# Staging the output weight of linear attention over freed operands, by GpSimd's queue, in a two-branch mixer

## The chip, the cores and the metric

The kernel runs on one core of one Trainium2 chip. The metric is the device time of one execution in microseconds (us); before the change three runs gave a median of 617.96 us, the lowest 616.56 and the highest 618.06.

## What is computed

From one input x of 2048 rows and 512 columns the reference computes `x + A(layernorm(x)) + B(layernorm(x))`, everything in float32. A is linear attention with 32 heads of 16 columns, B a gated MLP that mixes over the rows:

```python
# A: linear attention with a learned feature map
q, k, v = split(x @ wqkv)
phi_q = concat(softmax(q @ w_phi), softmax(-q @ w_phi))      # phi_k in the same way
kv, z = phi_k^T v, sum over rows of phi_k
o = (phi_q kv) / (phi_q z + 1e-6)
A = o @ wo                                                    # wo: 512 x 512
# B: gated MLP
z1, z2 = halves of gelu(x @ w_in)                             # 688 columns each
g = w_sp @ layernorm(z2) + b_sp
B = (z1 * g) @ w_out                                          # w_out: 688 x 512
```

## The kernel before

Every float32 operand of a matmul is split into a rounded high part and a rest (`round_h` on ACT, `rest_l` on DVE), and `mm3` issues three matmuls for one product. Rows are worked in 16 blocks of 128. A first stage projects q, k and v, forms the softmax features and adds up kv and z; the unnormalised q features of each block go to DRAM (`e_d`), as do the z1 halves (`z1_d`). A second stage makes z2 and splits it into the right operands B of the spatial product. A third stage computes `w_sp @ z2` in 8 pairs of output blocks times 4 quarters of the sum (`SEQ`, `products`); a drain (`drain`, L801 to L814) takes the sums out of PSUM, `gate` multiplies them with gelu(z1), and the transposed result u goes to DRAM. In the last pair the quarters run in the order 1, 2, 3, 0, so that the right operands of the second quarter (number 1) are dead first and those of the first quarter (number 0) last.

The last stage works on the blocks two at a time, i = 0, 2, ... 14. `project_u` multiplies u by w_out (tile `pout`), `attend` multiplies the features with kv and splits the outcome into `oT`, `project_o` multiplies `oT` with wo into the same `pout` and stores it: for most blocks ACT copies it to `xr` and GpSimd's queue adds it to the output, which already holds x (L1041). `features(s)` finishes the q features of block s: `q_fin` (L560 to L571) on DVE, from a load by `load_q` (tile `et`, L557). Blocks below 8 are turned by PE (`ptq`, L989), the later ones by DVE and a way through DRAM, which brings them back in pairs (`f`, L954). `ahead(i)` issues loads and features some blocks ahead.

What the change touches:

- SBUF is a stack. The right operands B of the third stage lie in tiles of one pool after another: the first quarter's in the pool `xz2a` and the first two tiles of `xz2`, the second quarter's in the last three tiles of `xz2` and in others. `stage_w` (L876) puts the raw rows of w_out into three tiles of `xz2` as they come free and splits them (tiles `wof` and `wu`, L49 and L53). When the third stage closes, the pool `cw` of the last stage takes the same addresses, in the order in which its tiles are first named (L961 to L967); a tile waits only for the users of the addresses under it.
- The raw rows of wo (tiles `wof`, one for each of 4 quarters of 128 rows) are loaded at L1056 to L1058 by SP, in 4 pieces of 32 rows each, so 16 DMAs, and split at once into `woh` and `wol`. The block at L1055 keeps ACT's and DVE's splits behind the split of u of block 1 (`uh`, `ul`) and behind `q_fin` of block 2 on their engines.
- Behind the wo loads (`load_w.last`) the block at L1059 puts, on SP, the features' load of block 3 (et(3)), the u of blocks 2 and 3, and et(4). `features(3)` follows `attend(0)` on DVE.
- `load_z1(7)`, the last pair's z1, is written at L1097 in step i = 2 and sent by GpSimd. The block around it names `lasts[6]`, an instruction of DVE (the last of `features`), and such a block orders only instructions of the same engine; so nothing holds the load back on GpSimd's queue.
- `er_pair` gives the pairs of turned features from a tag with 3 buffers.

The order on each engine is otherwise made by a planner, which simulates the program and takes what is ready first; instructions then run in that order on their engine or queue.

Of the kernel before, what the change touches and what calls it, by code (L numbers as in the profile page):

```python
# [10 lines left out]
F32 = mybir.dt.float32  # L11
F32R = mybir.dt.float32r
AF = mybir.ActivationFunctionType
ALU = mybir.AluOpType
# [4 lines left out]
P = 128  # L19
S, D, H, DH, FH = 2048, 512, 32, 16, 688  # L20
NT = S // P
ND = D // P
FC = FH // 2
NG = 4
NF = 2 * D
KF = FH // P
# [8 lines left out]
HP, QP = P // 2, P // 4  # L35
FP = 3 * P
# [5 lines left out]
def mixer(ctx: ExitStack, tc: tile.TileContext, x, x_t, wv, wqkT, phi_bd, wo, w_in, wst, b_r, w_out, out):  # L42
    nc = tc.nc
    pe, act, dve, pool, sp = nc.tensor, nc.scalar, nc.vector, nc.gpsimd, nc.sync


    def round_h(eng, h, src):
        if eng is act:
            return act.activation(h, src, AF.Copy).ins  # L49
        return eng.tensor_copy(h, src).ins  # L50

    def rest_l(l, src, h, eng=None):
        return (eng or dve).tensor_tensor(l, src, h.bitcast(F32), op=ALU.subtract).ins  # L53

    def mm3(dst, a, b, start, stop):
        (ah, al), (bh, bl) = a, b
        pe.matmul(dst, ah, bh, start=start, stop=False)  # L57
        pe.matmul(dst, ah, bl, start=False, stop=False)  # L58
        return pe.matmul(dst, al, bh, start=False, stop=stop).ins  # L59
# [12 lines left out]
    def xz_tile(n, dt, name):  # L72
        return xz.tile([P, SL], dt, tag="xz", name=name)[:, :n]
# [121 lines left out]
    with ExitStack() as p0:  # L195
# [16 lines left out]
        def split_w(h, l, src, t):  # L212
            sp.dma_start(t, src)
            round_h(act, h, t)
            rest_l(l, t, h)
# [134 lines left out]
        def proj_k(s):  # L350
            er = (spare[s] or stage("er")).rearrange("p a b -> p (a b)")[:, :NF + 2 * H] if s in spare else None
            return softmax_pair(wk, proj(s, wqk_h[:, 1], wqk_l[:, 1]), "k", r_x[:, s:s + 1], er=er)
# [79 lines left out]
        t = xz_tile(2 * D, F32R, "xT").rearrange("p (a b) -> p a b", a=2)  # L432
# [8 lines left out]
        for cs, pt in zip(halves, pts):  # L441
            src = pt.rearrange("p a b -> p (a b)")
# [63 lines left out]
        for s in range(NT):  # L506
# [6 lines left out]
            er = ek[s] if s < len(ek) else proj_k(s)  # L513
# [46 lines left out]
    def q_fin(et, tmp, zb):  # L560

        e, r, t, w = et[:, :NF], *(et[:, NF + k * 2 * H:NF + (k + 1) * 2 * H] for k in range(3))
        den = et[:, NF + 6 * H:QW]
        dve.tensor_tensor(tmp, e, zb, op=ALU.mult)
        dve.tensor_reduce(t, heads(tmp), axis=AX.X, op=ALU.add)
        dve.tensor_tensor(t, t, r, op=ALU.mult)
        dve.scalar_tensor_tensor(den, pairs(t, 0), EPS_DEN, pairs(t, 1), op0=ALU.add, op1=ALU.add)
        dve.reciprocal(den, den)
        dve.tensor_tensor(w.rearrange("p (h a) -> p h a", a=2), r.rearrange("p (h a) -> p h a", a=2),
                          den.unsqueeze(2).to_broadcast([P, H, 2]), op=ALU.mult)  # L570
        return e, dve.tensor_tensor(heads(e), heads(e), bc(w, 2 * H), op=ALU.mult).ins  # L571
# [6 lines left out]
    def turn_q(s, dst, e, eng):  # L578

        dve.transpose(dst.rearrange("p (m c t) -> p m c t", c=NB, t=BL), e.rearrange("p (c m j) -> p m c j", c=NB, j=BL))  # L580
        for b in range(P // BL):
            eng.dma_start(q_d[s, :, b * QB:(b + 1) * QB].rearrange("(m j) w -> j m w", j=BL),
                          dst[b * BL:(b + 1) * BL].rearrange("p (m w) -> p m w", w=QB))
# [154 lines left out]
    for s in range(NT):  # L738
# [8 lines left out]
        for k, q in p:  # L747
            ins = act.activation(z[(slice(None), *k)], q, AF.Gelu_apprx_tanh, scale=r_x[:, s:s + 1]).ins
# [95 lines left out]
    def slot(name, dt=F32):  # L844
        return xz_tile(2 * FH, dt, name)

    def load_w(src, parts, h, l, t):
        rows = 0
        for r0, r1 in parts:
            load_w.last = sp.dma_start(t[rows:rows + r1 - r0], src[r0:r1, :]).ins  # L850
            rows += r1 - r0
        return round_h(act, h, t[:rows]), rest_l(l, t[:rows], h)

    def load_u(i, u, rt):
        sp.dma_start(u, u_d[i])
# [18 lines left out]
    lasts, wu = [None] * 9, []  # L874

    def stage_w():  # L876
        t = [xz2.tile([P, SL], F32, tag="b", name="wof") for _ in range(3)]
        w = [xz_tile(2 * D, F32R, "wu") for _ in range(KF + 1)]
        for c in range(KF + 1):
            n = P if c < KF else 2 * REM  # L880
            h, l = (w[c][:n, k * D:(k + 1) * D] for k in range(2))
            rows = [(c * P, (c + 1) * P)] if c < KF else [(KF * P, FH)] * 2
            load_w(w_out, rows, h, l, t[c // 2][:, c % 2 * D:(c % 2 + 1) * D])
            wu.append((h, l))

    g, es, ets, ft, brought = {}, {}, {}, {}, {}
    for n in range(NC):
# [4 lines left out]
        if n % NQ == NQ - 1 and i < NP - 1:  # L892
            c = gt.tile([P, 2, FU], F32, tag="c", name="c")
# [7 lines left out]
        if n % NQ == NQ - 1 and i < NP - 1:  # L901
# [3 lines left out]
            if i in (2, 4):  # L905
                s = i // 2 - 1
                e, t = (gt.tile([P, 2, FU], F32, tag=tag, name=name).rearrange("p k f -> p (k f)")[:, :NF]
                        for tag, name in (("c", "c"), ("z1", "z1t")))
                pool.dma_start(e, e_d[s, :, :NF])
                turn_q(s, t, e, pool)  # L910
        if n == NC - 4:
            stage_w()
# [6 lines left out]
        if n == NC - 2:  # L919
# [4 lines left out]
            t = xz_tile((KF + 1) * P, F32R, "u1")  # L924
# [9 lines left out]
    cw = ctx.enter_context(left("cw", 1))  # L934
# [4 lines left out]
        return load_u(i, cw.tile([P, KF * P], F32, tag="u", bufs=4, name="u"),  # L939
                      cw.tile([2 * REM, P], F32R, tag="rt", bufs=6, name="rt"))  # L940

    def er_pair(name):
        return cw.tile([P, 2, NF], F32, tag="er", bufs=3, name=name)

    def features(s):
        with tc.issue_after(fin[-1]):
            tmp = slot("qtmp")[:, :NF]
            es[s], ins = q_fin(ets.pop(s), tmp, zb)
        fin.append(ins)
        if s >= TQ:  # L950
            if s % 2 == 0:
                ft[s] = er_pair("f")
            turn_q(s, tmp, es.pop(s), pool)
            brought[s] = sp.dma_start(ft[s - s % 2][:, s % 2], q_d[s]).ins  # L954
            return
        lasts[6] = ins

    def gated(u):
        return split_u(*u, wk.tile([P, KF, P], F32R, tag="uh", name="uh"), wk.tile([P, KF, P], F32R, tag="ul", name="ul"))

    er_pair("er")  # L961
    wo_h = cw.tile([P, ND, D], F32R, name="woh")
    cw.tile([2 * REM, P], F32R, tag="rt", bufs=6, name="rt")
    cw.tile([P, D], F32, tag="wof", bufs=4, name="wof")
    kvT = cw.tile([P, 2 * NG, HP], F32, name="kvT")
    cw.tile([P, KF * P], F32, tag="u", bufs=4, name="u")
    wo_l = cw.tile([P, ND, D], F32R, name="wol")  # L967
    with tc.issue_after(cb[1]), tc.issue_after(cb[2]):
        uT.append(gated(us.pop(1)))
    ctx_psg.__exit__(None, None, None)  # L970
# [50 lines left out]
    def project_o(i, oT, p):  # L1021
        ts = slice(i % 2 * P, (i % 2 + 1) * P)
        rows = slice(i * P, (i + 1) * P)
        xr = wk.tile([P, D], F32, tag="xr", bufs=3, name="xr")
        if i >= NT - 2:
            sp.dma_start(xr, x[rows, :])
        if i == NT - 1:
            dve.tensor_tensor(xr, p, xr, op=ALU.add)
            parts = [(slice(k * D // 2, (k + 1) * D // 2), pst.tile([P, D // 2], F32, tag="tr", name="pend")) for k in range(2)]
        else:  # L1030
            parts = [(slice(0, D), p)]
        for cs, q in parts:
            for c in range(ND):
                lasts[4] = mm3(q, (oT[0][:, c, ts], oT[1][:, c, ts]), (wo_h[:, c, cs], wo_l[:, c, cs]),
                               q is not p and c == 0, c == ND - 1)
            if i == NT - 2:
                dve.tensor_tensor(xr, p, xr, op=ALU.add)
                sp.dma_start(out[rows, :], xr)
            elif q is p:
                act.activation(xr, p, AF.Copy)  # L1040
                ins = pool.dma_start(out[rows, :], xr, accum_op=ALU.add).ins  # L1041
                tc.add_manual_dep(ins, seeds[i].name, mybir.DependencyInfo(
                    mybir.DependencyClass.Sync, mybir.DependencyReason.DATA), reason="out holds x")
            else:
                dve.tensor_tensor(xr[:, cs], q, xr[:, cs], op=ALU.add)
                sp.dma_start(out[rows, cs], xr[:, cs])
# [7 lines left out]
    wk.tile([P, NG, 2 * P], F32R, tag="oTh", name="oT")  # L1054
    with tc.issue_after(lasts[0]), tc.issue_after(lasts[1]), tc.issue_after(fin[-1]):  # L1055
        for c in range(ND):  # L1056
            rows = [(m * QP, (m + 1) * QP) for m in range(c // 2 * 8 + c % 2, (c // 2 + 1) * 8, 2)]
            load_w(wo, rows, wo_h[:, c], wo_l[:, c], cw.tile([P, D], F32, tag="wof", bufs=4, name="wof"))  # L1058
    with tc.issue_after(load_w.last):  # L1059
        ets[3] = load_q(3, slot("et"))  # L1060
        for s in (2, 3):
# [3 lines left out]
    def ahead(i):  # L1065

        if i + 5 < NT:
            ets[i + 5] = load_q(i + 5, slot("et"))
        if i + 4 < NT:
            with tc.issue_after(brought[i + 2]) if i + 6 >= NT else ExitStack():  # L1070
                us[i + 4] = fetch_u(i + 4)
        if 3 < i + 3 < NT:
            features(i + 3)
# [64 lines left out]
```

## Time and profile before

| what | value |
|---|---|
| median of the runs (lowest to highest) | 617.96 us (616.56 to 618.06) |
| the profiled execution's own time | 615.26 us |
| its span, first to last instruction | 613.6 us |
| PE busy | 606.3 us (99%) |
| DVE, ACT, POOL busy | 519.9, 259.9, 132.4 us |
| granted clock of PE | 1.00 |
| moved by DMA | 107.85 MB, mean 176 GB/s |

In the lines shown below, L49 is a cast to the high part, L53 the rest on DVE, L57 to L59 the three matmuls of `mm3`. A row of a timeline gives the start in us from the span's start, the length (of all, where rows are merged: x2, x4), engine and line, operation, tile written and tiles read, shapes, and in brackets how long the engine sat idle before it and what ended that. "SPq" is the queue of SyncE, whose rows are the issues of DMAs and not their transfers. Waits are given as total, times, longest. A row of a stretch gives from:to, its length, the busy time of PE, PEld, DVE, ACT and POOL with the number of instructions, PE's granted clock, the busy share of the 16 DMA engines and GB/s. A row of the DMA issues gives count, KB each and the median us from issue to landing.

### The profile page before, as it was taken

The numbers are of one execution on the slowest core, as the hardware profiler recorded it, in microseconds if no ns is written. First come the engines' busy times: TensorE is split into PE (matmuls) and PEld (weight loads), VectorE is DVE, ScalarE is ACT, GpSimd is POOL, SyncE is SP. The second block draws the span as 40 slices with busy tenths as digits, with TensorE's granted clock in tenths as the row PEclk, the third lists the DMA queues.
The fourth block names the chain that finished last, engine by engine and source line by source line (L and its number), as shares of the span: only waits on it lengthen the run. The fifth ranks groups of instructions, "written<-read, shape, count | busy, mean of one in ns | idle before, by whom it ended". The sixth has DMA issues, their size and how long they took to land.

```text
span 613.6 us, 11385 instructions
## 1 busy us (share of the span) xinstructions
PE 606.3 (99%) x4286; PEld 551.5 (90%) x4286; DVE 519.9 (85%) x930; ACT 259.9 (42%) x414; POOL 132.4 (22%) x231
## 2 busy tenths in 40 slices
PE   8999999999999999999999999999999999999997
PEld 7888888888888999999999999999999978777776
DVE  5999999999988588999989897787779979999932
ACT  5653334423433547887434443332435243332220
POOL 4122232333111014542000002001100131053440
PEclk9999999999999999999999999999999999999999
DMA  8557776666547848001454746455566798599882
GB/s 309 196 135 170 224 174 183 153 161 171 134 120 206 275 155 308 2 1 35 150 135 133 193 100 182 132 158 145 162 179 215 239 312 253 150 293 278 222 221 67
DMA packets 57950, 107.85 MB, mean 176 GB/s; under 512 B 12392, under 2 KB 24552, under 8 KB 57672
## 3 DMA queue, kind: packets, MB, share of 16 engines
q1 hardware_dynamic: 43656, 65.22, 34.5%
q0 software_dynamic: 11936, 36.28, 24.0%
q10 hardware_dynamic: 2304, 5.64, 2.4%
q8 instruction: 33, 0.54, 0.4%
q14 instruction: 21, 0.17, 0.1%
HBM read 66.85 MB, written 35.54 MB: 167 GB/s over the span
## 4 chain that ended last, share of the span: by engine, by line
PE 83%; DVE 6%; DMA 6%; issue 2%; SPq 1%; ACT 1%; POOL 0%; ACTq 0%; DVEq 0%; POOLq 0%
PE g L57 8%; PE g L58 8%; PE g L59 8%; PE proj L58 7%; PE proj L57 7%; PE proj L59 7%; PE zps L58 6%; PE zps L59 6%; PE zps L57 6%; PE pout L57 5%; PE pout L59 5%; PE pout L58 5%; DVE A L53 2%; DMA wf<-in_wst 1%; PE po L1004 1%
## 5 line engine op out<-in xcount | busy, mean ns | idle before, releaser
L57 PE MATMUL g<-B,A 128*128 128x344 f32 x448 | 142.5, 319 | 0.3 <-DVE c L810 0.3
L58 PE MATMUL g<-B,A 128*128 128x344 f32 x448 | 142.4, 319 | 0.0
L59 PE MATMUL g<-B,A 128*128 128x344 f32 x448 | 138.9, 318 | 0.0
L57 PEld LDWEIGHTS g<-B,A 128*128 128x128 f32 x448 | 84.0, 188 | 0.9 <-DVE c L810 0.6
L58 PEld LDWEIGHTS g<-B,A 128*128 128x128 f32 x448 | 84.0, 188 | 0.0
L59 PEld LDWEIGHTS g<-B,A 128*128 128x128 f32 x448 | 83.6, 188 | 0.0
L49 ACT ACTIVATE A<-S 128x512 fp32r<-128x512 f32 x64 | 39.4, 628 | 70.7 <-DVE S L622 52.3
L57 PE MATMUL proj<-wqk_h,xT 128*128 128x512 f32 x128 | 50.1, 391 | 0.0
L59 PE MATMUL proj<-wqk_h,xT 128*128 128x512 f32 x128 | 49.8, 389 | 0.0
L58 PE MATMUL proj<-wqk_l,xT 128*128 128x512 f32 x128 | 49.8, 389 | 0.0
L125 ACT ACTIVATE e<-e,r_x 128x1024 f32<-128x1024 f32 x26 | 29.8, 1149 | 42.3 <-DVE e L124 41.3
L53 DVE TENSOR_TENSOR A<-S,A 128x512 fp32r<-128x512 f32 x64 | 43.0, 684 | 3.0 <-ACT A L49 2.8
L49 ACT ACTIVATE A<-wf 128x512 fp32r<-128x512 f32 (+1 forms) x64 | 32.8, 515 | 28.1 <-DMA wf<-in_wst 15.8
L57 PE MATMUL zps<-w1h,xT 128*128 128x344 f32 (+2 forms) x128 | 40.8, 320 | 0.0
L59 PE MATMUL zps<-w1h,xT 128*128 128x344 f32 (+2 forms) x128 | 40.7, 318 | 0.0
L58 PE MATMUL zps<-w1l,xT 128*128 128x344 f32 (+2 forms) x128 | 40.7, 318 | 0.0
L57 PE MATMUL zps<-w2h,xT 128*128 128x344 f32 (+2 forms) x128 | 40.7, 318 | 0.0
L58 PE MATMUL zps<-w2l,xT 128*128 128x344 f32 (+2 forms) x128 | 40.6, 317 | 0.0
L59 PE MATMUL zps<-w2h,xT 128*128 128x344 f32 (+2 forms) x128 | 40.3, 317 | 0.0
L53 DVE TENSOR_TENSOR A<-wf,A 128x512 fp32r<-128x512 f32 (+1 forms) x64 | 35.1, 550 | 4.1 <-ACT A L49 4.0
L787 POOL DMA_DIRECT2D z1t<-z_d x16 | 8.7, 550 | 132.5 <-DMA wf<-in_wst 98.1
L128 DVE TENSOR_REDUCE sm<-e 128x64 f32<-128x1024 f32 x26 | 31.1, 1199 | 2.5 <-ACT e L125 2.5
(219 smaller groups left out, 1434.4 us busy)
## 6 DMA issues: line engine op xcount, KB each, us to landing
wf<-in_wst SPq DMA_DIRECT2D x64, 256.0 KB, 3.4
e_d<-e POOLq DMA_DIRECT2D x16, 544.0 KB, 5.0
et<-e_d SPq DMA_DIRECT2D x16, 544.0 KB, 7.6
z_d<-z1f ACTq DMA_DIRECT2D x16, 344.0 KB, 3.1
z1t<-z_d POOLq DMA_DIRECT2D x16, 344.0 KB, 4.6
zacc<-e POOLq DMA_DIRECT2D x10, 512.0 KB, 4.8
u<-u_d SPq DMA_DIRECT2D x15, 320.0 KB, 5.8
xt<-in_x SPq DMA_DIRECT2D x16, 256.0 KB, 4.4
```

The source lines that it names most:

```text
L49: return act.activation(h, src, AF.Copy).ins
L53: return (eng or dve).tensor_tensor(l, src, h.bitcast(F32), op=ALU.subtract).ins
L57: pe.matmul(dst, ah, bh, start=start, stop=False)
L58: pe.matmul(dst, ah, bl, start=False, stop=False)
L59: return pe.matmul(dst, al, bh, start=False, stop=stop).ins
L125: softmax_pair.last = less, act.activation(e, e, AF.Exp, scale=scale).ins
L128: dve.tensor_reduce(sm, heads(e), axis=AX.X, op=ALU.add)
L787: pool.dma_start(t[:, k, :FH], z1_d[2 * i + k])
L1004: lasts[3] = pe.matmul(po[r][c * QP:(c + 1) * QP, k], kvT[rows, m // 2, cols], fs[m // 4][rows, m // 2 % 2], start=True, stop=True).ins
```

## The change

The raw rows of wo get their place and their loads earlier in the code, right where the last stage's pools open. Three of the four quarters go out on GpSimd's queue (`eng=pool`), the last on SP's. The order of the tiles in `cw` is new: the pairs of turned features and the u buffers come first and lie over the first quarter's operands, as does `wol`; `wof` lies over two tiles in which the second quarter's operands lay, and after them the staging of w_out; `woh` lies over further tiles that the third stage has freed. `load_w` only loads, `split_w` only splits; the splits of wo stay where they were. The pairs of turned features get 2 buffers instead of 3. `lasts[6]` is now the last adding store of the output on GpSimd's queue, so that the last z1 load is queued behind it.

```diff
-    def load_w(src, parts, h, l, t):
+    def load_w(src, parts, t, eng=sp):
         rows = 0
         for r0, r1 in parts:
-            load_w.last = sp.dma_start(t[rows:rows + r1 - r0], src[r0:r1, :]).ins
+            load_w.last = eng.dma_start(t[rows:rows + r1 - r0], src[r0:r1, :]).ins
             rows += r1 - r0
-        return round_h(act, h, t[:rows]), rest_l(l, t[:rows], h)
+        return t[:rows]
+
+    def split_w(h, l, t):
+        return round_h(act, h, t), rest_l(l, t, h)
...
-            load_w(w_out, rows, h, l, t[c // 2][:, c % 2 * D:(c % 2 + 1) * D])
+            split_w(h, l, load_w(w_out, rows, t[c // 2][:, c % 2 * D:(c % 2 + 1) * D]))
...
-    def er_pair(name):
-        return cw.tile([P, 2, NF], F32, tag="er", bufs=3, name=name)
+    def f_pair():
+        return cw.tile([P, 2, NF], F32, tag="f", bufs=2, name="f")
...
-        lasts[6] = ins
...
-    er_pair("er")
-    wo_h = cw.tile([P, ND, D], F32R, name="woh")
+    f_pair()
+    cw.tile([P, KF * P], F32, tag="u", bufs=4, name="u")
     cw.tile([2 * REM, P], F32R, tag="rt", bufs=6, name="rt")
+    wo_l = cw.tile([P, ND, D], F32R, name="wol")
+    cw.tile([P, FP], F32, name="pad")
     cw.tile([P, D], F32, tag="wof", bufs=4, name="wof")
     kvT = cw.tile([P, 2 * NG, HP], F32, name="kvT")
-    cw.tile([P, KF * P], F32, tag="u", bufs=4, name="u")
-    wo_l = cw.tile([P, ND, D], F32R, name="wol")
+    wo_h = cw.tile([P, ND, D], F32R, name="woh")
+    wof = []
+    for c in range(ND):
+        rows = [(m * QP, (m + 1) * QP) for m in range(c // 2 * 8 + c % 2, (c // 2 + 1) * 8, 2)]
+        wof.append(load_w(wo, rows, cw.tile([P, D], F32, tag="wof", bufs=4, name="wof"), pool if c < ND - 1 else sp))
...
-                ins = pool.dma_start(out[rows, :], xr, accum_op=ALU.add).ins
+                lasts[6] = ins = pool.dma_start(out[rows, :], xr, accum_op=ALU.add).ins
...
         for c in range(ND):
-            rows = [(m * QP, (m + 1) * QP) for m in range(c // 2 * 8 + c % 2, (c // 2 + 1) * 8, 2)]
-            load_w(wo, rows, wo_h[:, c], wo_l[:, c], cw.tile([P, D], F32, tag="wof", bufs=4, name="wof"))
+            split_w(wo_h[:, c], wo_l[:, c], wof[c])
```

More of the change, by code (lines that the diff above doesn't have):

```diff
@@ L951, in features @@
             if s % 2 == 0:
-                ft[s] = er_pair("f")
+                ft[s] = f_pair()
             turn_q(s, tmp, es.pop(s), pool)
```

## The prediction

> **What bounds the kernel now.** I read the page first, then the list of PE's waits, then the timelines of PE, DVE, SP and POOL around 470 to 505 us, where the change lies, and last the stretches that show the DMA engines.
>
> ```profile
> span 613.6 us, 11385 instructions
> PE 606.3 (99%) x4286; PEld 551.5 (90%) x4286; DVE 519.9 (85%) x930; ACT 259.9 (42%) x414; POOL 132.4 (22%) x231
> ```
>
> PE is busy for 606.3 of 613.6 us. No edit here takes away a matmul, so the change can only win what PE idles where the edit acts, and it can lose whatever new wait it makes. The waits of PE from 480 us on:
>
> ```profile
> PE ptq L989 <- DVE et L571: 1.0, 1, 1.0
> PE pout L57 <- ACT oT L49: 0.2, 1, 0.2
> PE pout L57 <- DVE c L810: 0.2, 1, 0.2
> ```
>
> These are all. The timeline gives their places and sizes:
>
> ```profile
> 486.81 0.47 PE L57 MATMUL pout<-wu,u_uh 128*128 128x512 f32 x1 [0.16 <-DVE c L810]
> ...
> 496.26 0.50 PE L57 MATMUL pout<-woh,oT 128*128 128x512 f32 x1 [0.18 <-ACT oT L49]
> ...
> 503.52 1.53 PE L989 MATMUL ptq<-ident,et 128*128 128x128 f32 x12 [1.04 <-DVE et L571]
> ```
>
> So 1.38 us in all are to be had in the last stage: 0.16 + 0.18 + 1.04. Who made PE late is read on DVE:
>
> ```profile
> 470.43 1.29 DVE L53 TENSOR_TENSOR wu<-wof,wu 128x512 fp32r<-128x512 f32 x2
> ...
> 476.00 0.68 DVE L53 TENSOR_TENSOR wu<-wof,wu 96x512 fp32r<-96x512 f32 x1
> ...
> 479.63 1.23 DVE L564 TENSOR_TENSOR qtmp<-et,zb 128x1024 f32<-128x1024 f32 x1 [0.34 <-DMA et<-e_d]
> ...
> 483.28 1.23 DVE L571 TENSOR_TENSOR et<-et 128x1024 f32<-128x1024 f32 x1
> 484.43 0.57 DVE L805 SCALAR_TENSOR_TENSOR c<-g,bias,c 128x344 f32<-128x344 f32 x1
> ...
> 486.14 0.52 DVE L810 TENSOR_TENSOR c<-g,c 128x344 f32<-128x344 f32 x1
> ...
> 489.90 0.78 DVE L53 TENSOR_TENSOR ul<-u,uh 128x640 fp32r<-128x640 f32 x1
> 490.60 1.28 DVE L53 TENSOR_TENSOR wol<-wof,woh 128x512 fp32r<-128x512 f32 x2
> ...
> 495.75 0.69 DVE L53 TENSOR_TENSOR wol<-wof,woh 128x512 fp32r<-128x512 f32 x1 [2.57 <-ACT woh L49]
> 496.36 1.28 DVE L53 TENSOR_TENSOR oT<-po,oT 128x512 fp32r<-128x512 f32 x2
> 498.58 1.23 DVE L564 TENSOR_TENSOR qtmp<-et,zb 128x1024 f32<-128x1024 f32 x1 [0.94 <-DMA et<-e_d]
> ```
>
> Two chains stand here. The later one: the last quarter of wo comes late (2.57 us of idle DVE behind ACT's woh), so oT and then `features(3)` are late, and `features(3)` waits 0.94 us more for its own load, et(3). It runs from 498.58 to 503.5 and PE waits 1.04 us for it. The earlier one: `q_fin` of block 2 begins at 479.63, 0.34 us late, when et(2) lands; the drain of the last products (L805 to L810) stands behind it on DVE with no idle time in between, and PE's first pout matmul waits for L810. So the landing of et(2) already sets PE's start of the last stage.
>
> The queues behind both:
>
> ```profile
> 473.36 0.32 SPq L557 DMA_DIRECT2D et<-e_d  x1
> ...
> 480.60 11.54 SPq L850 DMA_DIRECT2D wof<-in_wo  x16
> 492.24 0.41 SPq L557 DMA_DIRECT2D et<-e_d  x1
> ```
>
> ```profile
> 479.41 1.07 POOL L787 DMA_DIRECT2D z1t<-z_d  x2 [23.89 <-DVE ul_rt L53]
> 490.01 2.35 POOL L837 DMA_DIRECT2D u_d<-z1t  x4 [9.53 <-DVE z1t L833]
> 492.35 2.25 POOL L839 DMA_DIRECT2D ur_d<-z1t  x4
> ...
> 520.53 0.86 POOL L1041 DMA_DIRECT2D out<-xr  x1 [0.78 <-ACT xr L1040]
> ```
>
> **What the change removes.** SP loses 12 of its 16 wo issues, 11.54 x 12/16 = 8.7 us of its queue, and et(3) stands right behind the sixteen. The four that stay take about 2.9 us, so et(3) goes out at about 483.5 instead of 492.24.
>
> ```profile
> et<-e_d SPq DMA_DIRECT2D x16, 544.0 KB, 7.6
> ...
> z1t<-z_d POOLq DMA_DIRECT2D x16, 344.0 KB, 4.6
> ```
>
> With 7.6 us to landing (the first row of the page's DMA issues) it is there at 491.1. wo itself: its staging now lies where stage_w's first staging tiles were. The first of those is free when DVE has split two quarters of w_out (470.43 + 1.29 = 471.7), the last when the remainder is split (476.00 + 0.68 = 476.7). POOL has nothing to do from 455 to 479.41 and issues a DMA in 0.54 us (1.07 for two). Twelve take 6.5 us: eight from 471.7 to 476.0, four from 476.7 to 478.9. How soon they land:
>
> ```profile
> DMA to landing us min/median/max: 3.2/4.6/6.4
> DMA to landing us min/median/max: 2.0/3.7/5.4
> ```
>
> The first row is of POOL's z1 loads (L787), the second of SP's wof loads (L850). Even 478.9 + 6.4 = 485.3 lies before ACT can take woh at all, since those casts stay queued behind the last uh:
>
> ```profile
> 485.82 0.74 ACT L49 ACTIVATE uh<-u 128x640 fp32r<-128x640 f32 x1 [4.33 <-DMA u<-u_d]
> ```
>
> ACT then does four woh, each smaller than this uh of 0.74 us, by 486.56 + 4 x 0.74 = 489.5, and DVE four wol from 490.60 in 4 x 0.64 = 2.6 us, to 493.2, oT in 1.28 to 494.5, and `features(3)` in the 4.9 us from 498.58 to 503.5 that it takes now: done at 499.4. PE needs it at 503.52 - 1.04 - 0.18 = 502.3, so 2.9 us are spare, and what is late next on DVE is nothing until there. Both stalls go: **-1.22 us**. The cover is those 2.9 us; if et(3) lands over 2.9 us behind 494.5, at 497.4, the stall returns one to one.
>
> **What the change moves.** z1's two loads leave POOL's place at 479.41 and go behind the second out store of step i = 2, to about 521.4. The out store ahead is not delayed; the next things on POOL are later stores, 1.07 us of issue later at most. The reader of z1 is the Gelu in the gate:
>
> ```profile
> 546.53 1.34 ACT L819 ACTIVATE z1t<-z1t 128x1376 f32<-128x1376 f32 x1
> ```
>
> 521.4 + 1.07 + 6.4 = 528.9, so 17 us are spare. Cost zero, as long as the transfers there do not starve DVE. The last of these rows is that stretch, the other three are used below:
>
> ```profile
> 469.00:471.00 2.00, 2.00 (x14) 2.00 (x13) 2.00 (x6) 2.00 (x5) 0.00 (x0) 1.00 0.93 312
> ...
> 473.00:479.00 6.00, 6.00 (x41) 6.00 (x40) 6.00 (x13) 3.96 (x8) 0.00 (x0) 1.00 0.97 308
> 479.00:486.00 7.00, 7.00 (x46) 7.00 (x45) 6.34 (x11) 0.64 (x2) 1.07 (x2) 1.00 0.99 300
> 518.00:527.00 9.00, 9.00 (x76) 7.07 (x75) 8.62 (x14) 4.60 (x9) 1.72 (x2) 1.00 0.88 211
> ```
>
> There the DMA engines are 0.88 busy and PE waits for nothing; if these 2 x 344 KB pushed one feature load back, DVE has the 2.9 us gained above.
>
> The f pairs get two slots instead of three. The third pair's first load would then wait for the first pair's reader:
>
> ```profile
> 555.86 1.09 PE L1004 MATMUL po<-f,kvT 64*32 64x256 f32 x32
> ...
> 565.06 8.38 SPq L954 DMA_DIRECT2D f<-q_d  x2
> ```
>
> The reader of the first pair is done at 557.0, and the third pair's first load is the second of the two in the SP row, which ends at 573.4: 16 us spare, zero. The u buffers now lie over the first quarter's operands, free only with the last products at 486.81 - 0.16 = 486.65, so SP can hold until then at the u loads; these stand behind et(3), which today goes out at 492.24, so they still go out earlier than today. Zero. wol also lies there, but is written at 490.60.
>
> **What it adds: traffic ahead of et(2).** This is the open cost. In 473 to 479 the DMA engines are 0.97 busy with SP's loads alone, et(2) among them, and et(2) decides when PE starts the last stage. Each wo issue carries 32 rows of 2 KB, 65.5 KB. The rate for such rows is that of 469 to 471, mostly w_out rows: 312 / 0.93 = 335 GB/s, or 0.195 us for one issue. Idle room is 0.03 x 6 = 0.18 us. From below: nothing that stands ahead of et(2) on SP is taken away, so it lands no earlier; the delay x is at least 0. From above: all sixteen go ahead, 16 x 0.195 - 0.18 = 2.9 us. By the release times above, the first wo quarter is surely ahead (four issues, 0.60 us), the second if it gets a slot in the same first staging tile (eight, 1.38 us); the other two are issued after 476.7, when et(2) is nearly done. I cannot see the slots and take the middle of one and two quarters, **x = 1.0 us**, added in full to the first wait of PE, for DVE has no idle time between et(2) and L810.
>
> The Trainium skill, "DMA: Bandwidth & Descriptors", section "Issuing engines are not separate DMA queues", says that DMAs started by SP, ACT and GpSimd run on the same 16 engines and interleave, so that spreading them saves issue time alone. By that rule the early bytes are paid for in full, the sum with two quarters ahead is +0.2 us, and the trace agrees: with POOL's z1 beside SP in 479 to 486 the rate is 300 GB/s at 0.99, with SP alone 308 at 0.97.
>
> **Sum.** -1.22 + 1.0 = -0.2 us. The profiled execution took 615.26 us (its span and 1.7 around it), 2.7 below the median of 617.96; I carry the difference over: 617.96 - 0.2 = 617.7 us. About 0.3%, 1.85 us, is what a measurement of this kernel can tell from no change.
>
> **Rivals.**
>
> *Only the gain (616.7 us).* If wo's packets take nothing from et(2), the whole 1.22 us stay: 617.96 - 1.22 = 616.7. That would come about if POOL's issues are held up while DVE runs, since DVE is busy for all of 473 to 479: wo would then be issued from DVE's gap at 479.3, be there by 479.3 + 6.5 + 6.4 = 492.2, late for the first wol by 1.6 us but inside the 2.9 us. The Trainium skill, "SBUF — State Buffer", section "SBUF: two separate sides", tells of such a lock between a two-port DVE instruction and GpSimd's descriptor writing. Against it: the u_d row has four POOL issues in 2.35 us, 0.59 each, while DVE runs the L53 rows from 489.90 on. For it also: how two queues share the engines when one has larger rows, as et(2) has, no row here shows. Chance 0.25.
>
> *Slower through et(2).* If three or four quarters go ahead of et(2), by slots that come free earlier than I think or by the fourth quarter being queued on SP before et(2), x is 12 x 0.195 - 0.18 = 2.2 to 2.9 us and the net +1.0 to +1.7: 618.9 to 619.7 us. It turns to a loss from x = 1.22, that is (1.22 + 0.18) / 0.195 = 7.2 issues ahead. For it: 0.97 busy engines and no idle DVE behind et(2). Against it: SP's order has et(2) at 473.36, before most of the space is free. Chance 0.15.
>
> *wo behind the u_d stores on POOL.* Then its twelve are issued from 492.35 + 2.25 = 494.6 to 501.1, the last lands at 505.7, and PE waits some 9 us at its first woh matmul: 9 - 1.2 gives about 625.8. Against it: z1, written much later in the code than those stores, stands ahead of them on POOL. Chance 0.03.
>
> *The staging is not free early.* If wo had to wait for the last products at 486.65, the last POOL issue would be at 493.1, its landing at 497.7 (4.6 us, the median), and woh, wol and oT (0.74 + 0.64 + 1.28) done at 500.4, where oT is done at 497.6 now. PE has no room there and waits the 2.8 us, `features(3)` shifts with it, and only the 1.04 us at ptq are won: +1.7, so 619.7. Chance 0.04.
>
> My forecast has 0.53. The range 616.2 to 619.6 holds it, most of the two near rivals and the scatter of single medians (616.56 to 618.06). Faster by over 0.3% needs the gain alone and some 0.6 us of scatter: 0.12. Slower by over 0.3% (past 619.8) has the u_d rival and, with some scatter, half of the other two slow ones: 0.13. Within: 0.75.
>
> **What would show it.** Right: POOL issues wof at 472 to 479, SP's et(3) is out by 485, no wait at ptq and at the first woh matmul, but the wait of the first pout on L810 is near 1.2 us and DVE idles about 1.3 us before the L564 at 480. Wrong: that L564 still begins at 479.6 (only the gain), begins after 481.6 (slower), POOL's wof stands behind u_d, or the ptq wait is still there.

## The result: slower, by a wait that the prediction did not have

The changed kernel takes 620.69 us (median of 6 runs, 620.03 to 621.69); the kernel before, run beside it, 616.35 us (6 runs, 615.79 to 618.06). The ratio is 1.0065, with a 95% interval of 1.0047 to 1.0083. The forecast was 617.7 with a range up to 619.6. The profiled execution took 620.42 us.

The profile after, first the page's line of the engines and PE's whole list of waits (total, times, longest):

```profile
span 618.7 us, 11393 instructions
PE 608.6 (98%) x4286; PEld 553.5 (89%) x4286; DVE 520.0 (84%) x930; ACT 259.8 (42%) x414; POOL 137.9 (22%) x243
```

```profile
PE pout L57 <- ACT oT L49: 4.8, 1, 4.8
PE idle L402 <- POOL ident masks.py:199: 1.8, 1, 1.8
PE pz L650 <- DVE zhl L53: 0.3, 1, 0.3
```

The three stalls of the last stage are gone (none is left over 0.15 us): those of 0.18 and 1.04 us as forecast, that of 0.16 us against the forecast, which had it grow by 1.0 us. In their place stands one of 4.8 us, before the first product with wo. Its cause is on ACT. These are the last of its cast rows before the change, where `oT` followed the last woh at once:

```profile
495.09 0.63 ACT L49 ACTIVATE woh<-wof 128x512 fp32r<-128x512 f32 x1 [2.63 <-DMA wof<-in_wo]
495.62 1.07 ACT L49 ACTIVATE oT<-po 128x512 fp32r<-128x512 f32 x2
```

And these are the rows after it:

```profile
486.29 0.74 ACT L49 ACTIVATE uh<-u 128x640 fp32r<-128x640 f32 x1 [4.85 <-DMA u<-u_d]
486.93 1.22 ACT L49 ACTIVATE woh<-wof 128x512 fp32r<-128x512 f32 x2
491.40 1.15 ACT L49 ACTIVATE woh<-wof 128x512 fp32r<-128x512 f32 x2 [3.25 <-DMA wof<-in_wo]
499.68 1.08 ACT L49 ACTIVATE oT<-po 128x512 fp32r<-128x512 f32 x2 [7.13 <-DMA ur_d<-z1t]
```

woh is done at 492.55, so wo is not what is late. `oT` then waits 7.13 us for a DMA that *reads* `z1t`: a store, of which `oT` needs nothing but the place. The queues and DVE show which of the prediction's other steps came. GpSimd's wo loads begin at 476.67 (forecast 471.7) and end at 483.98 (forecast 478.9); et(3) goes out at 485.24 (forecast 483.5, before the change 492.24); et(2) is not late; the z1 load stands behind the out stores:

```profile
476.67 3.94 POOL L850 DMA_DIRECT2D wof<-in_wo  x8 [21.86 <-DVE wu L53]
...
483.48 0.50 POOL L850 DMA_DIRECT2D wof<-in_wo  x1 [0.37 <-DMA wof<-in_wo]
489.27 1.77 POOL L837 DMA_DIRECT2D u_d<-z1t  x3 [5.30 <-DVE z1t L833]
...
493.29 0.58 POOL L839 DMA_DIRECT2D ur_d<-z1t  x1
...
527.48 1.48 POOL L787 DMA_DIRECT2D z1t<-z_d  x2
```

```profile
485.24 0.34 SPq L557 DMA_DIRECT2D et<-e_d  x1
```

```profile
478.92 1.21 DVE L564 TENSOR_TENSOR qtmp<-et,zb 128x1024 f32<-128x1024 f32 x1
...
492.07 1.29 DVE L53 TENSOR_TENSOR wol<-wof,woh 128x512 fp32r<-128x512 f32 x2 [0.92 <-ACT woh L49]
500.31 1.29 DVE L53 TENSOR_TENSOR oT<-po,oT 128x512 fp32r<-128x512 f32 x2 [6.95 <-ACT oT L49]
501.52 1.22 DVE L564 TENSOR_TENSOR qtmp<-et,zb 128x1024 f32<-128x1024 f32 x1
```

The eight stores of `z1t` (u of the last but one pair) land 5.5 to 7.4 us after their issue; the last is issued at 493.29 and lands 6.1 us later, at 499.4. `oT` starts at 499.68. Where `oT` lies explains the wait. In 4-byte columns of a partition, from the addresses of the two built programs: the pool `cw` ends at 42992 before the change and at 41328 after it, 1664 columns earlier, because the pairs of turned features take 2 x 2048 columns instead of 3 x 2048 and the new `pad` takes 384. Behind `cw` on the stack lies `cwk`, with `uh`, `ul`, `f`, `xr`, the unused tile `gap` and `oT`. All of it moves down. The high half of the first `oT` lay at 50288 to 51312, behind `z1t`, which is at 48624 to 50096; now it lies at 48624 to 49648, on it.

The second part of the loss comes right after the wait. Stretches of the changed kernel (from:to, length, busy PE, PEld, DVE, ACT, POOL, then PE's granted clock):

```profile
495.00:499.00 4.00, 0.53 (x3) 0.09 (x1) 0.00 (x0) 0.00 (x0) 0.00 (x0) 1.00 1.06 362
499.10:502.50 3.40, 2.17 (x5) 1.78 (x6) 2.19 (x3) 2.34 (x4) 0.00 (x0) 0.50 1.01 363
502.50:505.90 3.40, 3.40 (x9) 2.63 (x9) 3.19 (x7) 0.00 (x0) 0.00 (x0) 0.50 0.15 61
505.90:509.00 3.10, 3.10 (x17) 2.52 (x17) 3.09 (x4) 0.85 (x2) 0.97 (x1) 1.00 0.27 93
```

PE idles in the first row and gets half its clock in the next two. PE's timeline gives the price:

```profile
500.93 0.63 PE L58 MATMUL pout<-wol,oT 128*128 128x512 f32 x1
501.36 0.63 PE L57 MATMUL pout<-woh,oT 128*128 128x512 f32 x1
...
505.62 0.54 PE L58 MATMUL pout<-wol,oT 128*128 128x512 f32 x1
506.00 0.40 PE L59 MATMUL pout<-woh,oT 128*128 128x512 f32 x1
506.24 0.39 PE L57 MATMUL pout<-woh,oT 128*128 128x512 f32 x1
```

From 500.93 on twelve matmuls start 0.43 us apart; the thirteenth starts at 506.00, and from there they start 0.23 us apart. That is 506.00 - 500.93 = 5.07 us for twelve steps, and 5.07 - 12 x 0.23 = 2.3 us lost. Wait and half clock together are 7.1 us.

### The profile page after: what moved, and what is told of

It reads as the page before. It is cut to its first block, busy times and chain, and to the rows that moved or that the text cites. A ratio compares the mean times of both kernels' runs of the same rounds, so it can differ in the third digit from the quotient of the medians.

```text
span 618.7 us, 11393 instructions
## 1 busy us (share of the span) xinstructions
PE 608.6 (98%) x4286; PEld 553.5 (89%) x4286; DVE 520.0 (84%) x930; ACT 259.8 (42%) x414; POOL 137.9 (22%) x243
## 4 chain that ended last, share of the span: by engine, by line
PE 77%; DVE 11%; DMA 6%; issue 3%; ACT 1%; POOL 1%; SPq 0%; ACTq 0%; DVEq 0%; POOLq 0%
PE proj L57 7%; PE proj L58 7%; PE proj L59 7%; PE zps L57 6%; PE zps L59 6%; PE zps L58 6%; PE g L57 5%; PE g L58 5%; PE g L59 5%; PE pout L57 5%; PE pout L58 5%; PE pout L59 5%; DVE A L53 3%; DMA wf<-in_wst 2%; DMA z1t<-z_d 1%
```

## The experiments

The theory after the result was this: `oT` was moved onto `z1t` and waits for its stores, and the idle time halves the clock. The rivals: wo or GpSimd's queue makes `oT` late; the bytes ahead of et(2) cost something after all; the half clock has another cause; the moved z1 load does it. Ratios are to the kernel before, run beside each of them.

| kernel | wo | last z1 load | first `oT` | ratio, 95% interval | PE's waits over 0.15 us, 480 to 525 us |
|---|---|---|---|---|---|
| changed | new | held back | on `z1t` | 1.0065, 1.0047 to 1.0083 | 4.8 (oT) |
| a_gap | new | held back | off it | 0.9936, 0.9917 to 0.9956 | none |
| f_z1_later | as before | held back | off it | 0.9936, 0.9916 to 0.9956 | none |
| h_f_ot | as before | held back | on it | 1.0060, 1.0032 to 1.0088 | 6.0 (oT) |
| b_ot_on_z1t | as before | as before | on it | 1.0043, 1.0021 to 1.0065 | 2.9 (oT) |
| c_busy | new | held back | on it | 1.0090, 1.0062 to 1.0117 | 0.2, 2.8 (oT) |
| e_z1_early | new | early, ahead of wo | off it | 1.0014, 0.9997 to 1.0032 | 2.2 (oT) |
| e2_z1_behind | new | early, behind wo | off it | 0.9942, 0.9923 to 0.9961 | none |
| g2_wo_ahead | new, earlier | held back | off it | 0.9943, 0.9923 to 0.9963 | none |
| d_wo_sp | new place, SP | held back | off it | 0.9944, 0.9923 to 0.9964 | 1.1 (attend) |
| i_z1_half | as before | one of two held back | off it | 0.9963, 0.9944 to 0.9981 | 0.2, 0.4, 0.7 |

**oT off z1t, nothing else changed (a_gap).**

```diff
-    wk.tile([P, 10 * QP], F32, tag="gap", name="gap")
+    wk.tile([P, 36 * QP], F32, tag="gap", name="gap")
```

> The changed kernel with only the unused tile gap made 1664 columns larger, so that the tiles behind the shorter cw lie where they lay before the change (the first oT at column 50288 again, off z1t). My theory: ACT's oT waited 7.13 us for the eight stores of z1t alone, since oT lay on z1t; with oT off it, oT starts right behind the last woh (about 492.6), PE has no wait over 0.3 us from 480 us on, the clock stays at 1.00, and the three old stalls (0.16, 0.18, 1.04) stay away: about 1.2 to 1.4 us below the kernel before, some 615 where that one has 616.35, and 5 to 6 below the changed kernel. Rival, wo or GpSimd's queue is late: nothing moves with the addresses, PE still waits about 4.8 us for oT and the time stays at 620 to 621. Rival, the traffic ahead of et(2) (my prediction's x): a wait of about 1 us at the first pout and a time of about 616.2.

The order of the instructions on every engine is that of the changed kernel. ACT's timeline:

```profile
489.43 1.16 ACT L49 ACTIVATE woh<-wof 128x512 fp32r<-128x512 f32 x2 [1.24 <-DMA wof<-in_wo]
491.90 1.09 ACT L49 ACTIVATE oT<-po 128x512 fp32r<-128x512 f32 x2 [1.31 <-PE po L1011]
```

`oT` now waits for its own sums (`po`, from PE) alone. The kernel's span is 611.4 us, 7.3 below that of the changed kernel, against the 7.1 counted above. So one unused tile, made larger, turns 0.65% slower into 0.64% faster. The address is the cause; wo's lateness and the bytes ahead of et(2) are not.

**oT onto z1t in the kernel before (b_ot_on_z1t), and with the z1 load held back (h_f_ot).** Both leave out the same two lines:

```diff
-    wk.tile([P, 10 * QP], F32, tag="gap", name="gap")
-    wk.tile([P, NG, 2 * P], F32R, tag="oTh", name="oT")
```

> The kernel before, with the two unused tiles gap and the first oTh left out, so that its first oT lies at columns 49648 to 50672, on the end of z1t (48624 to 50096); nothing else is changed. My theory: ACT's oT then waits for the stores of z1t, which landed at 499.94 in the kernel before; it starts at about 500.0 instead of 495, PE waits 4 to 5 us for it, and after that the clock is granted at half for some 7 us, which costs about 2.6 us more; the 1.04 us at ptq go, since et(3) is in time by then. In all 5 to 6 us over the kernel before: 621.5 to 622.5. Rival, the loss belongs to wo's new place or queue: this kernel has neither and stays at 616.4.

> The kernel before with the last z1 load held back as in the changed kernel, and with the unused tiles gap and first oTh left out, so that its first oT lies at 49648 to 50672, on the end of z1t (48624 to 50096). wo stays on SP. That held-back load alone gave 0.9936 of the kernel before; there woh is cast by 491.9, oT at once after, and the eight stores of z1t land at 500.19. My theory: oT now waits for these stores until about 500, PE idles about 5 us for it where it idled not at all, and the clock is then granted at half for some 7 us, about 2.5 us more: 7 us over the kernel with the z1 load held back alone, ratio to the kernel before about 1.004 to 1.006. (The kernel before with oT on z1t could not show it: wo itself came so late there, woh until 498.49, that the stores, landed at 497.94, were no longer the last.) Rival, the loss of the changed kernel is wo's new place or queue: no wait, ratio about 0.994.

The first did not settle it. PE waited 2.9 us and the clock was halved for 3.4 us after it, but ACT's rows show that the wait ended with wo there and not with the stores: `oT` follows the last woh at once.

```profile
497.86 0.63 ACT L49 ACTIVATE woh<-wof 128x512 fp32r<-128x512 f32 x1 [2.36 <-DMA wof<-in_wo]
498.40 1.07 ACT L49 ACTIVATE oT<-po 128x512 fp32r<-128x512 f32 x2
```

Why wo came 2.8 us later there than in the kernel before (497.86 against 495.09) stays open. The second has wo early, and it came as expected, in a kernel that holds no part of wo's move: PE waits 6.0 us, its clock is halved for 6.8 us (498.4 to 505.3), and the span is 619.3 us, 8.2 above that of the kernel with the held-back load alone.

```profile
491.36 0.63 ACT L49 ACTIVATE woh<-wof 128x512 fp32r<-128x512 f32 x1 [1.84 <-DMA wof<-in_wo]
501.07 1.09 ACT L49 ACTIVATE oT<-po 128x512 fp32r<-128x512 f32 x2 [9.08 <-DMA ur_d<-z1t]
```

**PE's idle time filled (c_busy).** The changed kernel and 18 matmuls more, whose result nobody reads:

```diff
+            busy = pst.tile([P, ND, P], F32, tag="tr", name="busy")
+            with tc.issue_after(lasts[2]):
+                for k in range(18):
+                    pe.matmul(busy[:, k % ND], ident, ident, start=True, stop=True, skip_group_check=True)
```

> The changed kernel with 18 idle matmuls of 128x128 on PE (0.24 us each, 4.3 us in all) between the last u product and the first woh product of the last stage, where PE waits 4.8 us for oT. My theory says that the half clock from 499.10 to 505.93 follows from PE's idling: with the idle time filled, oT still starts at about 499.7, the clock stays at 1.00, the matmuls behind take 0.23 us apart instead of 0.43, and about 2.6 us are saved against the changed kernel: about 618. Rival, the half clock has another cause: it is granted all the same, and the time stays at 620 to 621 or rises.

The time rose where the theory had it fall. But the planner answered the added matmuls with another order on DVE, SP and GpSimd, in which `oT` of the next step is late, so that the time tells nothing of the clock. The stretches do:

```profile
497.00:501.50 4.50, 4.42 (x38) 4.17 (x36) 0.00 (x0) 0.50 (x2) 0.00 (x0) 1.00 1.05 380
501.70:505.10 3.40, 3.40 (x14) 2.48 (x15) 3.37 (x4) 1.73 (x4) 0.00 (x0) 1.00 0.56 225
518.00:522.20 4.20, 1.57 (x7) 0.94 (x5) 4.20 (x5) 0.72 (x1) 0.00 (x0) 1.00 0.14 26
522.23:525.64 3.41, 3.25 (x8) 2.58 (x9) 3.31 (x8) 0.00 (x0) 0.00 (x0) 0.50 0.30 93
```

`oT` is late here too (PE's first product with it starts at 501.65), but PE was kept busy, and the clock behind it is 1.00. Where PE idled 2.8 us, ahead of 522.39, the clock is halved. So the half clock follows PE's idle time, wherever that comes from. What filling the gap would save in time stays unmeasured.

**The z1 load alone (f_z1_later).** The kernel before with this one edit:

```diff
-        lasts[6] = ins
...
-                ins = pool.dma_start(out[rows, :], xr, accum_op=ALU.add).ins
+                lasts[6] = ins = pool.dma_start(out[rows, :], xr, accum_op=ALU.add).ins
```

> The kernel before with one part of the change alone: the last z1 load is held back until behind the out stores of step i = 2, as in the changed kernel. wo stays on SP, all tiles stay where they were. By my prediction this part is worth nothing by itself (its reader is 17 us away, and the stall at ptq comes from SP's wo issues ahead of et(3)): within 0.3 us of the kernel before, with 1.0 us still waited at ptq. Rival, z1's 344 KB twice in 479 to 486 take DMA time from wo and et(3): wo lands up to 2 us earlier, the waits at the first woh product and at ptq go, and the time falls by up to 1.2 us.

The rival came true, and the gain is larger than it asked for. PE waits for nothing from 480 us on; the span is 611.1 us. SP's waits, first in the kernel before, then here (both from 478 to 494 us), show how:

```profile
SPq L850 <- DMA u<-u_d: 2.4, 1, 2.4
```

```profile
SPq L850 <- DMA u<-u_d: 0.5, 1, 0.5
```

SP's wo loads stand behind the load of u of block 1, and the sixth of them, the ninth issue counted from that load, was held until it had landed. The sixteen took 11.54 us of SP's queue in the kernel before; here they take 8.13:

```profile
480.40 8.13 SPq L850 DMA_DIRECT2D wof<-in_wo  x16
```

In the kernel before u lands at 485.8, when ACT's `uh` starts; without z1's 688 KB beside it at 483.2:

```profile
483.22 0.74 ACT L49 ACTIVATE uh<-u 128x640 fp32r<-128x640 f32 x1 [1.92 <-DMA u<-u_d]
...
491.30 0.63 ACT L49 ACTIVATE woh<-wof 128x512 fp32r<-128x512 f32 x1 [2.33 <-DMA wof<-in_wo]
```

The last woh starts at 491.30 instead of 495.09. The gain of the median (617.73 to 613.29, 4.4 us) is larger than that of the profiled spans (613.6 to 611.1, 2.5 us), and of the 2.5 us only 1.38 are the three waits. The runs' clocks account for a part of the rest: 12 of the 23 runs of the kernel before had a mean granted clock of 0.996 or 0.997, and all six of this kernel 0.999 or 1.000. Half a clock for 3.4 us is 3.4 x 0.5 / 613 = 0.28%, so in about half of its runs the kernel before seems to have its clock halved once. But those 12 runs have a median of 618.43 us and the other 11 one of 616.93, which is still 3.6 us above this kernel's. The one profile shown, of 615.26 us, is of a run near the fast end. Longer waits than its own, too short to halve the clock (2.2 us were, in e_z1_early below), would explain the 11; no trace of such a run of the kernel before was kept, so this is not shown.

**wo moved, z1 not (e_z1_early), and z1 behind wo (e2_z1_behind).** From a_gap. Both take `lasts[6]` away from the out store, as shown; the first gives it back to the last instruction of `features`, as in the kernel before, the second to wo's last load on GpSimd's queue:

```diff
-                lasts[6] = ins = pool.dma_start(out[rows, :], xr, accum_op=ALU.add).ins
+                ins = pool.dma_start(out[rows, :], xr, accum_op=ALU.add).ins
```

> The changed kernel with oT off z1t, and the last z1 load no longer held back: wo alone is moved. GpSimd issues it behind wo, at about 484. My theory now: in the kernel before, z1's 688 KB were taken out of the same DMA time as wo, which made wo late; who comes first decides. Here wo is first and lands by about 489 to 491, so PE has no wait for woh or at ptq, and the time is about the same as with the load held back: ratio 0.993 to 0.996. Rival, the held-back load wins by leaving this stretch altogether: z1's bytes, 2.3 us of DMA time, then delay et(3), u and the stores instead, a wait of 1 to 2 us comes up somewhere before 505, and the ratio is 0.997 to 1.000.

The expectation had the queue's order wrong. The planner put z1 ahead of wo, and GpSimd's seventh and eighth wo load were held behind z1's two (again the ninth issue from the load waited for):

```profile
479.36 1.07 POOL L787 DMA_DIRECT2D z1t<-z_d  x2 [24.36 <-DVE ul_rt L53]
480.43 2.97 POOL L850 DMA_DIRECT2D wof<-in_wo  x6
484.61 0.50 POOL L850 DMA_DIRECT2D wof<-in_wo  x1 [1.21 <-DMA z1t<-z_d]
486.99 0.50 POOL L850 DMA_DIRECT2D wof<-in_wo  x1 [1.88 <-DMA z1t<-z_d]
```

wo's last loads go out up to 489.8, and PE waits 2.2 us for `oT`. With z1 ahead of it wo's move wins nothing.

> The changed kernel with oT off z1t and z1's two loads on GpSimd right behind its twelve wo loads, at about 484 (without a held-back load the planner had put them ahead of wo, at 479.36, and PE waited 2.2 us for oT). My theory: whoever stands first gets the DMA time; wo, ahead now, lands by 490 to 491 and woh, wol and oT wait for nothing. z1's 688 KB then fall on et(3), the u loads and the stores of z1t, which has some 3 us to spare at ptq: waits under 1 us, ratio 0.994 to 0.998. Rival, z1's load has to leave the stretch altogether: et(3) or u is late by 2.3 us or more and PE waits over 1 us, ratio 0.999 to 1.002.

Here z1 is issued at 487.34, behind wo, PE waits for nothing from 480 us on, and the ratio is that of the kernels with the load held back. z1 need not leave the stretch; it must not stand ahead of wo.

**wo's bytes ahead of et(2) (g2_wo_ahead).** From a_gap, with `pad` and `wof` moved in `cw` so that wo's staging begins at column 35312, and `gap` adjusted to keep `oT` in place:

> The changed kernel with oT off z1t, and wo's staging moved to column 35312, so that its first two quarters lie on the staging tile of w_out's second half, which is split before 475, and the last two partly on the remainder's (476.4). It measures the term x of my prediction, wo's bytes ahead of et(2). By the prediction: GpSimd issues eight loads before 476, x = 8 x 0.195 - 0.18 = 1.4 us at most: L564 of et(2) begins 1 to 1.4 us later and PE waits as long at its first pout: ratio 0.995 to 0.996 where the kernel with oT off z1t has 0.9936. Rival, wo's bytes take nothing from et(2), or the slots come free no earlier: the first pout waits less than 0.3 us and the ratio stays at 0.993 to 0.994.

```profile
475.38 1.99 POOL L850 DMA_DIRECT2D wof<-in_wo  x4 [19.30 <-PE g L59]
477.88 1.97 POOL L850 DMA_DIRECT2D wof<-in_wo  x4 [0.51 <-DVE wu L53]
```

```profile
480.36 1.23 DVE L564 TENSOR_TENSOR qtmp<-et,zb 128x1024 f32<-128x1024 f32 x1 [0.16 <-DMA et<-e_d]
```

Eight loads go out between 475.38 and 479.85, before et(2) is used. DVE starts on it 6.12 us after its issue at 474.24, with a wait of 0.16 us; in the kernel before, without these loads, it was 6.27 us after the issue, with a wait of 0.34. PE waits for nothing. The rival stands.

**wo's queue (d_wo_sp).** From a_gap, with all sixteen loads on SP: `pool if c < ND - 1 else sp` becomes `sp`.

> The changed kernel with oT off z1t and all 16 wo loads on SP instead of 12 on GpSimd: the place is the new one, the queue the old one. My theory: once z1's load is out of the way, neither place nor queue of wo decides; no wait over 0.3 us, ratio 0.993 to 0.995. Rival, GpSimd's queue is what the changed kernel gains by: SP's 12 more issues, 0.5 us each, put et(3) and the u loads 6 us back, and a wait of 1 us or more comes up at ptq: ratio over 0.996.

There is no wait at ptq. PE waits 1.1 us once, until 491.35, at the first matmul of `attend`. The profile puts that wait down to DVE's split of wol, which this matmul does not read. It does read kvT, whose load now stands behind the sixteen and goes out at 488.25, 7.9 us later than in the changed kernel; that this load is the cause is likely and not shown. The theory had no wait over 0.3 us; its ratio came all the same.

**Half of z1 (i_z1_half).** The kernel before with the second of z1's two loads held back:

> The kernel before with only the second of z1's two loads (344 KB each) held back until behind the out stores of step i = 2; the first stays where it was, at 479.4. With both early wo's last load lands at 494.62 and PE waits 0.18 and 1.04 us behind it; with both late it lands at 491.02 and PE waits for nothing. My theory: it is the bytes, so one load costs half: wo's last load lands at 492.5 to 493.2, the wait at ptq is 0 to 0.3 us, and the ratio to the kernel before lies between 0.9936 and 1, near 0.995. Rival, it is the presence of a second queue, whatever its bytes: wo lands at 494 and the ratio stays at 0.998 to 1.000. Rival, the second load alone does the harm: nothing is lost and the ratio is 0.9936.

This one is mixed. In the profiled run hardly anything is won: the last wof lands at 494.92, PE waits 0.16, 0.35 and 0.72 us, and SP's row reads

```profile
SPq L851 <- DMA u<-u_d: 3.0, 1, 3.0
```

So one load beside u makes u as late as two, and not half as late; the proportion by bytes fails. Yet the interval of the ratio excludes 1. All seven of its runs had a mean clock of 0.999 or 1.000, where 7 of the 12 of the kernel before beside them had 0.996 or 0.997. A part of what it gains seems to be the halved clock; but its median of 615.15 us also lies below the other 5 of those 12 (616.91). Where that comes from stays open.

## Why the prediction was wrong, point by point

- **The step that failed:** "The f pairs get two slots instead of three", priced at "16 us spare, zero". I asked of each tile in `cw` when its own address comes free and when its own reader runs, and took the pool's *length* for nothing. I applied the rule of the addresses to wo, and not to what lies behind `cw`. What the runs showed in its place: the shorter pool moved `oT` onto `z1t`, and that cost 4.8 us of waiting and 2.3 us of half clock. (The zero for the u buffers held: their next load goes out at 486.33, before the change at 492.69.) The wait could have been estimated, given the addresses: the prediction quotes four `ur_d` stores issued from 492.35 to 494.60, and PE's wait for `oT` ending at 496.26. `z1t` is read until the last of these stores has landed, and in that trace they landed 4.5 to 6.2 us after their issue, the last of which was at 494.04; so a tile laid on `z1t` could be written at 498.5 at the earliest. None of my rivals held this, and the range ended 1.1 us below the median measured.
- **The removal, -1.22 us:** right in which stalls go and when, not in what takes them away. With `oT` off `z1t` (a_gap) DVE writes `oT` from 492.84 to 494.12 (forecast 494.5), `features(3)` ends at 498.9 (forecast 499.4), and et(3) goes out at 483.98 (forecast 483.5). But the z1 load alone takes the same stalls away (f_z1_later), and wo's move with z1 ahead of it leaves PE a wait of 2.2 us for `oT` (e_z1_early); that the change held back z1 as well was luck, as far as this term goes. I took SP's row of sixteen issues in 11.54 us as issue time alone. 2.4 us of it were the wait for u, which z1's load made late. The size was missed too: without the wait for `z1t` the change wins 4.1 us of the median (617.73 to 613.66), for the reasons and with the open end given under f_z1_later.
- **z1's move, "Cost zero":** the sign was missed. It carries the whole gain of the change, 0.9936 alone, and wo's move adds nothing to it (a_gap, also 0.9936); moving z1 behind wo, to 487.34, is enough (e2_z1_behind). I asked whether z1 would be late behind the stores, and not who is delayed by it where it stood.
- **x = 1.0 us:** measured as none. The changed kernel's DVE starts L564 at 478.92 without idle time. GpSimd's first wo load goes out at 476.67, not 471.7, since the first slot lies on the remainder's staging; and with eight loads earlier (g2_wo_ahead) PE still waits for nothing. The prediction took "paid for in full" from the rule of the Trainium skill's page "DMA: Bandwidth & Descriptors" (section "Issuing engines are not separate DMA queues") that the DMAs of all issuing engines interleave on the same 16 engines. That rule does not say which of two loads pays: et(2), issued first, did not, while u of block 1 landed 2.6 us later with z1's loads beside it.
- **The rivals:** "only the gain" was right in its place (no delay of et(2)) and wrong in its reason: GpSimd issues a load every 0.50 us while DVE is busy. "wo behind the u_d stores" had the stores that did the harm, but by chance: it had wo wait for them in the queue, and not `oT` for their landing.

## What to carry to other kernels

When a tile of a stacked pool changes its size, list the addresses of everything behind it, in that pool and the next, before and after, and ask for each who used that place last; a DMA that only reads a dead tile counts as a user until it lands. When a bundle of edits is costed, cost the smallest one with the sign open: here the edit of two lines is the gain, and the rest adds nothing to it. The version to keep is the kernel before with the z1 load held back, 0.64% below it.

## What the runs showed of the hardware

- In these traces PE's clock was halved after an idle time of 2.8 us or more, and the price outlasts the wait. Idle for 4.8 us and 6.0 us it was granted 0.50 for 6.8 us, idle for 2.9 and 2.8 us for 3.4 us, idle for 2.2 us not at all. The limit need not be a sharp one: each figure is of one profiled run. The Trainium skill, "TensorE: Matmul & The Clock Gate", section "Part 1: The HAM clock gate (the "warmup" mystery)", tells of a free-running window of about 3.4 us and of half the clock after at least one idle window; the lengths of 3.4 and 6.8 us agree with the window, but 2.8 us of idle time, less than one window, were enough here.
- A queue's next issue can be held until an earlier load of the same queue has landed: SP's sixth wo load for 2.4 us behind u's in the kernel before, GpSimd's seventh and eighth for 1.21 and 1.88 us behind z1's in e_z1_early, by the profile's releasers. Each time the issue that was held is the ninth, counted from the load that it waited for. So a slow load delays what stands behind it on its queue. Whether the chip or the built program sets this limit, no run tells.
- Stores of small tiles can be slow to finish: 24 and 160 KB took 5.5 to 7.4 us from issue to landing in the changed kernel, with the DMA engines busy all the time in 491 to 502. In the kernel before the same stores took 2.9 to 6.2 us, with a busy share of 0.98 in that stretch; why they took longer after the change is open.
